# The last stage's sums of weight blocks, made once in memory by negating copies and adding DMA

## The chip, the cores and the metric

The kernel runs on one core of a Trainium2 chip. The time is the device time of one execution in microseconds; the times before are 738.42, 739.38 and 739.89 us, with a median of 739.38. The profile comes from one further execution, which took 738.09 us.

## The reference

The output is a gated mix of two branches over the same input `x` (1 x 2048 x 1024, bf16). Branch a is attention over eight earlier positions, two apart, with 32 heads of 32; branch b is a GELU-gated two-matrix layer with 3584 hidden columns.

```
def _A_ref(x, wqkv, wo):                 # H = 32; Dh = D // H; W, dil = 8, 2
    qkv = (x @ wqkv).reshape(B, S, 3, H, Dh)
    ...
    logits = jnp.einsum("bhsd,bhswd->bhsw", q, kg) * scale
    logits = jnp.where(mask[None, None, :, :], logits, -1e9)
    attn = _softmax(logits, axis=-1)
    o = jnp.einsum("bhsw,bhswd->bhsd", attn, vg)
    return (lambda x, *d: x.transpose(*d))(o, 0, 2, 1, 3).reshape(B, S, D) @ wo

def _B_ref(x, w_gate, w_up, w_down):
    g = jnp.einsum("bsd,df->bsf", x, w_gate)
    u = jnp.einsum("bsd,df->bsf", x, w_up)
    h = _gelu(g) * u
    return jnp.einsum("bsf,fd->bsd", h, w_down)

x = A_x
g = _sigmoid((x * gate_w).sum(-1, keepdims=True))
a = _A_ref(x, A_wqkv, A_wo)
b = _B_ref(x, B_w_gate, B_w_up, B_w_down)
return g * a + (1 - g) * b
```

The kernel puts `g` and `1 - g` into the attention weights and into `h`, so that both branches end in one matrix product: `[h, o]` (2048 x 4608) times `[w_down; wo]` (4608 x 1024). This product is the last stage, and the change is about its right-hand side.

## The kernel before

**Products with seven instead of eight block multiplications.** Every large product is cut into 2 x 2 blocks and made with seven block products and sums of blocks (the Strassen-Winograd scheme). The sums of right-hand blocks in the last stage are T1 = R12 - R11, T2 = R22 - T1, T3 = R22 - R12 and T4 = R21 - T2. A block R11, R12, R21 or R22 is a half of the 36 row blocks of `[w_down; wo]` (14 of `w_down`, 4 of `wo`) by 512 of the 1024 columns: 128 partitions x 18 x 512 in bf16, 2.36 MB. The first digit says which half of the rows, the second which half of the columns.

**Unit stage.** 78 units (class `Unit`, lines 354 to 407) make the gate and up products, q, k and v. A unit is 28 matmuls of 128x512 on TensorE. The loop at line 1005 goes through the units and writes each engine's order by hand: `p1` of the unit, `p73` of the one before, `p5`, `p26`, `p4` of the one before, then the callbacks of that iteration (`at`, before; `at_end`, after), and then `run_bg`, which gives VectorE and the DMA queues pieces of background work (attention, sums, stores). Within a unit ScalarE copies X to Y (L378), keeps V (L383), writes the first quarter to the unit's tile (L366 Gelu or L368 copy), copies Y to Z (L390) and writes another quarter; a gate unit ends with a Gelu of the second half (L405). TensorE adds onto Y and Z, so it waits for L378 and L390.

**Tiles of the units.** Gate and up units take their tiles from a ring of five (`st_tile`, lines 218 to 221). When a pair of a gate and an up unit is done, VectorE multiplies the two tiles (L250) and GpSimd stores the gate's tile to `h_d` in memory (L254). Gate units have even numbers from 28 on. The store of units n and n+1 is written in iteration n+3, and unit n+5 takes the same tile.

**Queues.** SP issues nearly all loads, in the order in which the program writes them. GpSimd issues the stores to `h_d`, `o_d`, `w_d` and others, likewise in order. A DMA that has to wait for data holds back what is behind it on its queue.

**Last stage.** `down(s)` runs twice, for 1024 rows of the output each time (s = 0, 1). A pass has seven block products of 72 matmuls each (L904) in this order: A11 x R11, A12 x R21, S x T1, S x T2, A12 x R22, A11 x T3, A22 x T4, where the left-hand blocks A and S are scaled and combined by VectorE (L831, L838, L950). The right-hand sums are made on VectorE by `comb_task` (L838): T1 over R11, T2 in a buffer of its own, T3 over R12, T4 (with a minus sign) over R21. `plan` says which of ten arena buffers of 18 KB each block lies in, for each pass. The four blocks R11, R21, R12 and R22 are loaded anew in the second pass (`loads_1` to `loads_6`). R11 is first loaded by a callback at unit 62 (`n - 16`), R21 while attention ends. The outputs of the first pass go out on GpSimd's queue, those of the second on SP's.

**The arena.** One tile holds everything in SBUF, by offsets in KB. 92 to 120 is used by the v projection's weights and sums until unit 25, and from unit 62 on by the last stage's buffers.

Of the kernel before, what the change touches and what calls it, by code (L numbers as in the profile page):

```python
# [46 lines left out]
R_ST = 178  # L47
R_P5B = 198.5
R_RAW = (0, 8)
R_S = (16, 24)  # L50
R_VB = 32
R_AB = 41
# [14 lines left out]
def kernel(  # L67
# [37 lines left out]
    def reg3(kb, a, b):  # L105
        return reg(kb, a * b).rearrange("p (a b) -> p a b", a=a)
# [14 lines left out]
    v_d = tc.dram_tile([P, NT, HALO + S], BF16, name="v_d")  # L121
    h_d = tc.dram_tile([P, 2 * NPAIR, S], BF16, name="h_d")
    o_d = tc.dram_tile([P, NT, S], BF16, name="o_d")
    z_d = tc.dram_tile([HK, S], F32, name="z_d")
    g_d = tc.dram_tile([2, S], BF16, name="g_d")
    w_d = tc.dram_tile([NBLK, 32, NJ, SC], BF16, name="w_d")
# [4 lines left out]
    with tc.manual_schedule(engines={mybir.EngineType.PE, mybir.EngineType.DVE, mybir.EngineType.Activation,  # L131
# [55 lines left out]
        def flat(a):  # L187
            return a.rearrange("p a b -> p (a b)")
# [605 lines left out]
        def load_A(b, s, half, c, i0, i1, with_o):  # L794
            t0 = s * SUP + c * SC
            nc.sync.dma_start(out=b[:, i0:i1, :], in_=h_src(half, t0, i0, i1))
            if with_o:
                nc.sync.dma_start(out=b[:, NH_:NK, :], in_=o_d[:, half * 4:half * 4 + 4, t0:t0 + SC])

        def h_src(half, t0, i0, i1):  # L800
            return h_d[:, :, t0:t0 + SC].rearrange("p (i two) s -> p i two s", two=2)[:, i0:i1, half, :]

        def load_R(b, half, nh):
            n0 = nh * SC
            nc.sync.dma_start(out=b[:, 0:NH_, :],
                              in_=B_w_down[:, n0:n0 + SC].rearrange("(i two p) n -> p i two n", two=2, p=P)[:, :, half, :])
            nc.sync.dma_start(out=b[:, NH_:NK, :],
                              in_=A_wo[:, n0:n0 + SC].rearrange("(p t) n -> p t n", t=NT)[:, 4 * half:4 * half + 4, :])

        plan = [dict(A11=4, R11=5, A12=2, R21=3, A21=6, A22=0, R12=1, R22=7, S=8, T2=9),  # L810
                dict(A11=6, R11=5, A12=8, R21=9, A21=2, A22=4, R12=7, R22=1, S=0, T2=3)]
        u2 = regf(R_U2, 4 * SC).rearrange("p (j n) -> p j n", j=4)
        qs = regf(R_QS, 4 * SC).rearrange("p (j n) -> p j n", j=4)
        on = [0]
# [8 lines left out]
        def Bs(s):  # L823
            return {k: bufs[v] for k, v in plan[s].items()}
# [9 lines left out]
        def comb_task(o_, a, b, op, step=4):  # L834
            for i0 in range(0, NK, step):
                i1 = min(NK, i0 + step)
                f = lambda t_: flat(t_[:, i0:i1, :])
                TT(out=f(o_), in0=f(a), in1=f(b), op=op)  # L838
                yield 0.05 + 0.273 * (i1 - i0)

        def run(*gens):
            for g in gens:
                for _ in g:
                    pass

        def pieces(*gens):
            for g in gens:
                yield from g

        def take(g, k):  # L850
            for _ in range(k):
                if next(g, None) is None:
                    break
# [19 lines left out]
        def loads_1(s):  # L873
            B = Bs(s)
            load_A(B["A11"], s, 0, 0, 0, NH_, True)
            load_R(B["R11"], 0, 0)

        def loads_2(s):
            B = Bs(s)
            load_A(B["A12"], s, 1, 0, 0, NH_, True)  # L880
            load_R(B["R21"], 1, 0)

        def loads_3(s):
            load_A(Bs(s)["A21"], s, 0, 1, 0, NH_, True)

        def loads_4(s):
            load_A(Bs(s)["A22"], s, 1, 1, 0, NH_, True)

        def loads_5(s):
            load_R(Bs(s)["R12"], 0, 1)  # L890

        def loads_6(s):
            load_R(Bs(s)["R22"], 1, 1)

        def down(s):
            B = Bs(s)
            last = s == 1
            eng = nc.sync if last else nc.gpsimd
            base = s * SUP
            XT, VT = (6, 7, 0, 1), (5, 2, 3, 4)  # L900

            def mm(ps, L, R, j, start, q0=0, q1=NK):
                for q, i in list(enumerate(KORD))[q0:q1]:
                    nc.tensor.matmul(ps, lhsT=L[:, i, j * P:(j + 1) * P], rhs=R[:, i, :], start=(start and q == 0),  # L904
                                     stop=(q == NK - 1), skip_group_check=not start)

            def emit(ot, c, nh, j):
                r0 = base + c * SC + j * P
                eng.dma_start(out=o2[r0:r0 + P, nh * SC:(nh + 1) * SC], in_=ot)

            def add_out(ps, t_, c, nh, j):
                ot = out_tile()
                TT(out=ot, in0=ps, in1=t_, op=ALU.add)  # L913
                emit(ot, c, nh, j)

            A11, A12, A21, A22 = B["A11"], B["A12"], B["A21"], B["A22"]
            R11, R12, R21, R22, S, T2 = B["R11"], B["R12"], B["R21"], B["R22"], B["S"], B["T2"]
            T1 = R11
            XP = [bank(XT[j]) for j in range(4)]
            VP = [bank(VT[j]) for j in range(4)]  # L920
            rest = pieces(scale_task(A21, s, 1, 0, NE_), scale_task(A22, s, 1, 0, NE_), comb_task(S, A21, A22, ALU.add))
            for j in range(4):
                if j > 1 or last:
                    mm(XP[j], A11, R11, j, True)
                else:
                    mm(XP[j], A11, R11, j, True, 0, NK - 2)
                    yield
                    if j == 1:
                        for jj in range(2):
                            mm(XP[jj], A11, R11, jj, True, NK - 2, NK)  # L930
                            nc.scalar.copy(out=u2[:, jj, :], in_=XP[jj])
                if j > 1 or last:
                    nc.scalar.copy(out=u2[:, j, :], in_=XP[j])  # L933
                take(rest, 3)
            run(rest)
            rest = comb_task(T1, R12, R11, ALU.subtract)
            for j in range(4):
                mm(XP[j], A12, R21, j, False)
                ot = out_tile()
                nc.scalar.copy(out=ot, in_=XP[j])  # L940
                emit(ot, 0, 0, j)
            run(rest)
            t2 = comb_task(T2, R22, T1, ALU.subtract)
            for j in range(4):
                mm(VP[j], S, T1, j, True)
                nc.scalar.copy(out=qs[:, j, :], in_=VP[j])
            run(t2)
            for j in range(4):
                js = slice(j * P, (j + 1) * P)
                TT(out=S[:, :, js], in0=S[:, :, js], in1=A11[:, :, js], op=ALU.subtract)  # L950
            run(comb_task(A12, A12, S, ALU.subtract), comb_task(A11, A11, A21, ALU.subtract))
            if not last:
                loads_1(1)
            rest = pieces(comb_task(R12, R22, R12, ALU.subtract), comb_task(R21, R21, T2, ALU.subtract))
            for j in range(4):
                mm(XP[j], S, T2, j, True)
                TT(out=u2[:, j, :], in0=XP[j], in1=u2[:, j, :], op=ALU.add)
                TT(out=qs[:, j, :], in0=qs[:, j, :], in1=u2[:, j, :], op=ALU.add)
                take(rest, 2)
            for j in range(4):  # L960
                mm(VP[j], A12, R22, j, False)
                add_out(VP[j], u2[:, j, :], 0, 1, j)
                take(rest, 1)
            run(rest)
# [12 lines left out]
            for j in range(4):  # L977
                mm(XP[j], A22, R21, j, False)
                add_out(XP[j], u2[:, j, :], 1, 0, j)
                take(rest, 1)  # L980
            run(rest)

        n = len(units)
# [2 lines left out]
        def run_last(b):  # L986
            now[0] = b
            prv = units[b - 1]
            for t_ in [t_ for t_ in tasks if t_.wake < b]:
                t_.finish()  # L990
            prv.p73()
            pre_down_3(0)
            loads_3(0)
# [66 lines left out]
```

## Time and profile before

| | |
|---|---|
| median of three runs | 739.38 us |
| profiled execution | 738.09 us |
| its span, first to last instruction | 736.3 us |
| TensorE busy | 724.4 us (98%) |
| VectorE busy | 589.6 us (80%) |
| ScalarE busy | 290.8 us (39%) |
| GpSimd busy | 91.3 us (12%) |
| DMA queue of SP (q1) | 77.41 MB, 34.4% of 16 engines' span |
| software DMA queue of GpSimd (q0) | 29.15 MB, 11.9% |
| granted TensorE clock | 1.000 |

The profile names engines PE (TensorE), DVE (VectorE), ACT (ScalarE), POOL (GpSimd) and SP. L904 means line 904 of the kernel before. Matmuls are pipelined and their ends are modelled, so the mean of one in a group (379 ns) is longer than the distance between two of them. The chain of waits is followed back from the last instruction: each step goes to what released it or to the instruction before it on its engine. The unit stage ends and the last stage begins around 517 us.

### The profile page before, as it was taken

The page shows a single profiled execution, that of the slowest core. Times are in us where ns is not written, and L with a number is a line of the kernel's source. Part 1 is how long each engine was busy: PE and PEld are TensorE (multiplying, and loading weights), DVE is VectorE, ACT ScalarE, POOL GpSimd, SP SyncE. Part 2 cuts the span into 40 slices and gives each one's busy share as a digit, 9 for nine tenths or more (in the row PEclk, how much of TensorE's full clock was granted, in tenths as well). Part 3 has the DMA queues.
Part 4 walks back from the last instruction along what each step waited for, and adds up shares of the span by engine and source line. Part 5 has one row for each costly group of instructions (what it writes and reads, how often), then busy time and mean ns, then how long its engine had stood idle before and what let it go on. Part 6 is the DMA issues. An engine that isn't in the chain of part 4 may idle for free.

```text
span 736.3 us, 9168 instructions
## 1 busy us (share of the span) xinstructions
PE 724.4 (98%) x3498; PEld 355.9 (48%) x3567; DVE 589.6 (80%) x626; ACT 290.8 (39%) x500; POOL 91.3 (12%) x160
## 2 busy tenths in 40 slices
PE   8999999999999999999999999999999999999998
PEld 4466665656544444444444444444444444444443
DVE  2697879878998899999999999986488944927921
ACT  4554445445566655555555555555110000110000
POOL 1222233411201100101001010000010011000000
PEclk9999999999999999999999999999999999999999
DMA  9972001362328334634346553637990899300011
GB/s 278 274 185 66 16 25 33 104 224 83 110 72 238 96 103 128 202 109 150 117 143 218 175 158 97 215 116 277 305 300 1 276 364 361 113 28 1 8 43 37
DMA packets 108333, 107.68 MB, mean 146 GB/s; under 512 B 17488, under 2 KB 95472, under 8 KB 108288
## 3 DMA queue, kind: packets, MB, share of 16 engines
q1 hardware_dynamic: 97856, 77.41, 34.4%
q0 software_dynamic: 10144, 29.15, 11.9%
q8 instruction: 28, 0.46, 0.3%
q10 hardware_dynamic: 288, 0.52, 0.3%
q14 instruction: 17, 0.14, 0.1%
HBM read 74.42 MB, written 30.55 MB: 143 GB/s over the span
## 4 chain that ended last, share of the span: by engine, by line
PE 81%; issue 1%; ACT 0%; DVE 0%
PE banks L360 51%; PE banks L904 29%; PE banks L596 1%; ACT L686 0%; DVE arena L913 0%; ACT arena L686 0%; ACT arena L366 0%; ACT banks L378 0%; ACT arena L405 0%
## 5 line engine op out<-in xcount | busy, mean ns | idle before, releaser
L360 PE MATMUL banks<-arena 128*128 128x512 bf16 x2137 | 472.2, 379 | 4.9 <-DVE arena L397 1.1
L360 PEld LDWEIGHTS <-arena 128*128 128x128 bf16 x2184 | 240.5, 111 | 236.1 <-issue 7.8
L904 PE MATMUL banks<-arena 128*128 128x512 bf16 x988 | 217.2, 379 | 1.1
L904 PEld LDWEIGHTS <-arena 128*128 128x128 bf16 x1008 | 98.6, 98 | 119.3 <-issue 0.6
L397 DVE TENSOR_TENSOR arena<-banks,arena 128x1024 bf16<-128x1024 f32 x78 | 95.2, 1221 | 39.3 <-PE banks L360 21.7
L383 ACT COPY arena<-banks 128x512 f32<-128x512 f32 x78 | 45.7, 586 | 130.9 <-PE banks L360 130.9
L730 DVE TENSOR_TENSOR arena<-arena 128x2048 bf16<-128x2048 bf16 x64 | 76.9, 1218 | 0.4
L368 ACT CAST arena<-banks 128x512 bf16<-128x512 f32 x102 | 59.7, 586 | 42.8 <-PE banks L360 42.8
L591 DVE TENSOR_TENSOR arena<-arena 128x2048 bf16<-128x2048 bf16 x64 | 74.7, 1218 | 0.1
L737 DVE TENSOR_TENSOR arena<-arena 128x2048 bf16<-128x2048 bf16 (+2 forms) x96 | 73.8, 775 | 1.1
L838 DVE TENSOR_TENSOR arena<-arena 128x2048 bf16<-128x2048 bf16 (+1 forms) x70 | 73.4, 1112 | 0.5 <-DMA arena<-in_B_w_down_dram 0.4
L913 DVE TENSOR_TENSOR arena<-banks,arena 128x512 bf16<-128x512 f32 x24 | 16.5, 690 | 47.6 <-PE banks L904 47.6
L390 ACT COPY banks<-banks 128x512 f32<-128x512 f32 x78 | 44.5, 571 | 22.1 <-PE banks L360 19.8
L254 POOL DMA_DIRECT2D h_d<-arena x28 | 20.1, 716 | 252.0 <-DVE arena L250 195.1
L378 ACT COPY banks<-banks 128x512 f32<-128x512 f32 x78 | 45.0, 577 | 13.8 <-PE banks L360 12.4
L317 DVE TENSOR_TENSOR arena<-arena 128x1024 bf16<-128x1024 bf16 x60 | 38.6, 685 | 0.5
L366 ACT ACTIVATE arena<-banks 128x512 bf16<-128x512 f32 x54 | 32.2, 597 | 15.2 <-PE banks L360 14.3
L250 DVE TENSOR_TENSOR arena<-arena 128x2048 bf16<-128x2048 bf16 x28 | 34.0, 1215 | 3.3 <-ACT arena L368 1.9
L831 DVE TENSOR_TENSOR arena<-arena,omgrep 128x2048 bf16<-128x2048 bf16 x24 | 28.1, 1217 | 10.4 <-DMA arena<-h_d 10.4
L933 ACT COPY arena<-banks 128x512 f32<-128x512 f32 x6 | 3.5, 586 | 81.8 <-PE banks L904 81.8
L950 DVE TENSOR_TENSOR arena<-arena 128x2304 bf16<-128x2304 bf16 x8 | 10.8, 1356 | 22.9 <-PE banks L904 20.3
L405 ACT ACTIVATE arena<-arena 128x1024 bf16<-128x1024 bf16 x27 | 28.3, 1049 | 0.0
(74 smaller groups left out, 256.8 us busy)
## 6 DMA issues: line engine op xcount, KB each, us to landing
h_d<-arena POOLq DMA_DIRECT2D x28, 512.0 KB, 4.0
arena<-in_B_w_down_dram SPq DMA_DIRECT2D x8, 1792.0 KB, 13.4
arena<-h_d SPq DMA_DIRECT2D x6, 1792.0 KB, 13.4
arena<-in_B_w_gate_dram SPq DMA_DIRECT2D x15, 512.0 KB, 5.2
arena<-in_B_w_up_dram SPq DMA_DIRECT2D x15, 512.0 KB, 4.3
arena<-in_A_wqkv_dram SPq DMA_DIRECT2D x6, 1024.0 KB, 10.8
arena<-v_d SPq DMA_DIRECT2D x8, 544.0 KB, 6.1
v_d<-arena POOLq DMA_DIRECT2D x16, 256.0 KB, 2.3
```

Of the source, the lines that this page charges most:

```text
L317: TT(out=o_, in0=a, in1=b_, op=op)
L360: self.pe = nc.tensor.matmul(ps, lhsT=self.L[form](kt), rhs=rhs[:, kt, :], start=(start and kt == 0), stop=(kt == HK - 1), skip_group_chec ...
L368: nc.scalar.copy(out=o_, in_=i_)
L378: nc.scalar.copy(out=self.Y, in_=self.X)
L383: nc.scalar.copy(out=self.p5s, in_=self.V)
L390: nc.scalar.copy(out=self.Z, in_=self.Y)
L397: TT(out=self.T[:, :, c2s], in0=pair, in1=self.p5s.rearrange("p (o n) -> p o n", o=1).to_broadcast([P, 2, SC]), op=ALU.add)
L591: TT(out=dst, in0=q.rearrange("p (o s) -> p o s", o=1).to_broadcast([P, NWIN, AC]), in1=_win_ap(k, [[-DIL, NWIN], [1, AC]]), op=ALU.mult)
L730: TT(out=prod2[(t // 2) % 2][:, t % 2], in0=ab, in1=_win_ap(v[:, t, HALO:HALO + AC], [[SJ, NJ], [-DIL, NWIN], [1, SJ]]), op=ALU.mult)
L737: TT(out=out_, in0=h(0), in1=h(1), op=ALU.add)
L838: TT(out=f(o_), in0=f(a), in1=f(b), op=op)
L904: nc.tensor.matmul(ps, lhsT=L[:, i, j * P:(j + 1) * P], rhs=R[:, i, :], start=(start and q == 0), stop=(q == NK - 1), skip_group_check=not ...
```

## The change

The four sums T1 to T4 are made once, in memory (`t_d`, four tensors of one block), during units 28 to 66, and both passes load them as blocks of their own.

- In units 28 to 54 SP loads the blocks R11, R12 and R22 in thirds (six row blocks, 0.786 MB) into four buffers at 92 to 116 KB of the arena. ScalarE negates them in place, 128x1024 at a time, one piece at the end of each of iterations 30 to 56. GpSimd stores the result: -R11 as the start of T1, -R12 as the start of both T2 and T3, -R22 as the start of T4.
- GpSimd then issues DMAs that add in memory: R12 to T1 (unit 41), R11 to T2 (50), R22 to T3 (52), R22 to T2 (56), R21 to T4 (60), each in two parts (`w_down` and `wo`), and at unit 66 T1 to T4.
- In the last stage the VectorE sums T1 to T4 and the load of R12 go away; T1 to T4 are loaded by SP. `plan` gives them buffers, and the loads of both passes are put at other places between the products.

```diff
+R_NEG = 92
+    t_d = [tc.dram_tile([P, NK, SC], BF16, name=f"t_d{k}") for k in range(4)]
...
+        def r_parts(half, nh, i0=0, i1=NK):
...
+        def load_T(b, k):
+            nc.sync.dma_start(out=b, in_=t_d[k - 1][:])
+
+        NP = 6
+        NQ = NK // NP
+        neg = [reg3(R_NEG + NP * q, NP, SC) for q in range(4)]
+
+        def neg_load(q, half, nh):
+            i0 = NP * (q % NQ)
+            for sl, src in r_parts(half, nh, i0, i0 + NP):
+                nc.sync.dma_start(out=neg[q % 4][:, sl.start - i0:sl.stop - i0, :], in_=src)
+
+        def neg_scale(q, r):
+            g = flat(neg[q % 4][:, 2 * r:2 * r + 2, :])
+            nc.scalar.activation(out=g, in_=g, func=ACT.Copy, scale=-1.0)
+
+        def neg_store(q, ks):
+            i0 = NP * (q % NQ)
+            for k in ks:
+                nc.gpsimd.dma_start(out=t_d[k - 1][:, i0:i0 + NP, :], in_=neg[q % 4])
+
+        def t_add(k, half, nh):
+            for sl, src in r_parts(half, nh):
+                nc.gpsimd.dma_start(out=t_d[k - 1][:, sl, :], in_=src, accum_op=ALU.add)
+
+        def t_add_t(k, k2):
+            nc.gpsimd.dma_start(out=t_d[k - 1][:], in_=t_d[k2 - 1][:], accum_op=ALU.add, max_dma_last_dim=2 * SC)
+
+        for q in range(3 * NQ):
+            half, nh, ks = ((0, 0, (1,)), (0, 1, (2, 3)), (1, 1, (4,)))[q // NQ]
+            at(28 + 3 * q, lambda q=q, half=half, nh=nh: neg_load(q, half, nh))
+            for r in range(3):
+                at_end(30 + 3 * q + r, lambda q=q, r=r: neg_scale(q, r))
+            at(33 + 3 * q, lambda q=q, ks=ks: neg_store(q, ks))
+        for n_, k, a in ((41, 1, (0, 1)), (50, 2, (0, 0)), (52, 3, (1, 1)), (56, 2, (1, 1)), (60, 4, (1, 0))):
+            at(n_, lambda k=k, a=a: t_add(k, *a))
+        at(66, lambda: t_add_t(4, 1))
...
-        plan = [dict(A11=4, R11=5, A12=2, R21=3, A21=6, A22=0, R12=1, R22=7, S=8, T2=9),
-                dict(A11=6, R11=5, A12=8, R21=9, A21=2, A22=4, R12=7, R22=1, S=0, T2=3)]
+        plan = [dict(A11=4, R11=5, A12=2, R21=3, A21=6, A22=0, S=8, T1=1, T2=9, R22=7, T3=5, T4=3),
+                dict(A11=6, R11=1, A12=8, R21=9, A21=2, A22=4, S=0, T1=7, T2=5, R22=3, T3=1, T4=9)]
...
-            rest = comb_task(T1, R12, R11, ALU.subtract)
+            loads(s, "T3")
             for j in range(4):
-                mm(XP[j], A12, R21, j, False)
+                mm(XP[j], A12, B["R21"], j, False)
...
-            run(rest)
-            t2 = comb_task(T2, R22, T1, ALU.subtract)
+            loads(s, "T4")
             for j in range(4):
-                mm(VP[j], S, T1, j, True)
+                mm(VP[j], S, B["T1"], j, True)
                 nc.scalar.copy(out=qs[:, j, :], in_=VP[j])
-            run(t2)
...
-                loads_1(1)
-            rest = pieces(comb_task(R12, R22, R12, ALU.subtract), comb_task(R21, R21, T2, ALU.subtract))
+                loads(1, "A11", "R11")
...
+                loads(1, "A12", "R21")
...
-                loads_2(1)
-                loads_3(1)
-                loads_5(1)
+                loads(1, "A21", "T1")
...
-                mm(XP[j], A11, R12, j, True)
+                mm(XP[j], A11, B["T3"], j, True)
...
-                loads_4(1)
-                loads_6(1)
+                loads(1, "A22", "T2")
...
+            if not last:
+                loads(1, "R22")
...
-            loads_4(0)
-            loads_5(0)
-            loads_6(0)
+            loads(0, "A22", "T1", "T2", "R22")
```

More of the change, by code (lines that the diff above doesn't have):

```diff
@@ L801, in h_src @@
             return h_d[:, :, t0:t0 + SC].rearrange("p (i two) s -> p i two s", two=2)[:, i0:i1, half, :]
-        def load_R(b, half, nh):
[L804 to L808, printed above, removed]
@@ L810 @@
-        plan = [dict(A11=4, R11=5, A12=2, R21=3, A21=6, A22=0, R12=1, R22=7, S=8, T2=9),
-                dict(A11=6, R11=5, A12=8, R21=9, A21=2, A22=4, R12=7, R22=1, S=0, T2=3)]
+        def r_parts(half, nh, i0=0, i1=NK):
+            ns = slice(nh * SC, (nh + 1) * SC)
+            if i0 < NH_:
+                e = min(i1, NH_)
+                yield slice(i0, e), B_w_down[:, ns].rearrange("(i two p) n -> p i two n", two=2, p=P)[:, i0:e, half, :]
+            if i1 > NH_:
+                a = max(i0, NH_)
+                yield slice(a, i1), A_wo[:, ns].rearrange("(p t) n -> p t n", t=NT)[:, 4 * half + a - NH_:4 * half + i1 - NH_, :]
@@ new lines, in load_R @@
+        def load_R(b, half, nh):
+            for sl, src in r_parts(half, nh):
+                nc.sync.dma_start(out=b[:, sl, :], in_=src)
+        def load_T(b, k):
[7 more added lines that the diff above has]
+                nc.sync.dma_start(out=neg[q % 4][:, sl.start - i0:sl.stop - i0, :], in_=src)
@@ new lines, in neg_scale @@
+        def neg_scale(q, r):
[6 more added lines that the diff above has]
+        def t_add(k, half, nh):
+            for sl, src in r_parts(half, nh):
+                nc.gpsimd.dma_start(out=t_d[k - 1][:, sl, :], in_=src, accum_op=ALU.add)
@@ L871, in pre_down_3, with loads @@
                 load_A(B[k], s, half, 0, NE_, NH_, False)
-        def loads_1(s):
+        def loads(s, *names):
             B = Bs(s)
[L875 to L893, printed above, removed]
+            for k in names:
+                if k[0] == "A":
+                    load_A(B[k], s, int(k[2]) - 1, int(k[1]) - 1, 0, NH_, True)
+                elif k[0] == "R":
+                    load_R(B[k], int(k[1]) - 1, int(k[2]) - 1)
+                else:
+                    load_T(B[k], int(k[1]))
         def down(s):
@@ L914, in add_out @@
                 emit(ot, c, nh, j)
-            A11, A12, A21, A22 = B["A11"], B["A12"], B["A21"], B["A22"]
-            R11, R12, R21, R22, S, T2 = B["R11"], B["R12"], B["R21"], B["R22"], B["S"], B["T2"]
-            T1 = R11
+            A11, A12, A21, A22, S = B["A11"], B["A12"], B["A21"], B["A22"], B["S"]
             XP = [bank(XT[j]) for j in range(4)]
@@ L923, in down @@
                 if j > 1 or last:
-                    mm(XP[j], A11, R11, j, True)
+                    mm(XP[j], A11, B["R11"], j, True)
                 else:
-                    mm(XP[j], A11, R11, j, True, 0, NK - 2)
+                    mm(XP[j], A11, B["R11"], j, True, 0, NK - 2)
                     yield
@@ L929, in down @@
                         for jj in range(2):
-                            mm(XP[jj], A11, R11, jj, True, NK - 2, NK)
+                            mm(XP[jj], A11, B["R11"], jj, True, NK - 2, NK)
                             nc.scalar.copy(out=u2[:, jj, :], in_=XP[jj])
@@ L952, in down @@
             if not last:
-                loads_1(1)
-            rest = pieces(comb_task(R12, R22, R12, ALU.subtract), comb_task(R21, R21, T2, ALU.subtract))
+                loads(1, "A11", "R11")
             for j in range(4):
-                mm(XP[j], S, T2, j, True)
+                mm(XP[j], S, B["T2"], j, True)
                 TT(out=u2[:, j, :], in0=XP[j], in1=u2[:, j, :], op=ALU.add)
                 TT(out=qs[:, j, :], in0=qs[:, j, :], in1=u2[:, j, :], op=ALU.add)
-                take(rest, 2)
+            if not last:
+                loads(1, "A12", "R21")
             for j in range(4):
-                mm(VP[j], A12, R22, j, False)
+                mm(VP[j], A12, B["R22"], j, False)
                 add_out(VP[j], u2[:, j, :], 0, 1, j)
-                take(rest, 1)
-            run(rest)
+            rest = pieces()
             if not last:
-                loads_2(1)
-                loads_3(1)
-                loads_5(1)
+                loads(1, "A21", "T1")
                 rest = pieces(scale_task(Bs(1)["A11"], 1, 0, 0, NE_), scale_task(Bs(1)["A12"], 1, 0, 0, NE_))
             for j in range(4):
-                mm(XP[j], A11, R12, j, True)
+                mm(XP[j], A11, B["T3"], j, True)
                 add_out(XP[j], qs[:, j, :], 1, 1, j)
@@ L974, in down @@
             if not last:
-                loads_4(1)
-                loads_6(1)
+                loads(1, "A22", "T2")
             for j in range(4):
-                mm(XP[j], A22, R21, j, False)
+                mm(XP[j], A22, B["T4"], j, False)
                 add_out(XP[j], u2[:, j, :], 1, 0, j)
                 take(rest, 1)
+            if not last:
+                loads(1, "R22")
             run(rest)
@@ L992, in run_last @@
             pre_down_3(0)
-            loads_3(0)
+            loads(0, "A21")
             first = down(0)
```

## The prediction

> **What bounds the kernel now.** I read the chain of waits first, then the groups for the last stage's lines, then the pieces of the chain where anything but TensorE stands in it, then the DMA busy share by stretch, then ScalarE and GpSimd in order of time.
>
> The page's chain and groups (group columns: busy us, mean ns of one, then idle us just before the group and who ended it):
>
> ```profile
> PE banks L360 51%; PE banks L904 29%; PE banks L596 1%; ACT L686 0%; DVE arena L913 0%; ACT arena L686 0%; ACT arena L366 0%; ACT banks L378 0%; ACT arena L405 0%
> ...
> L904 PE MATMUL banks<-arena 128*128 128x512 bf16 x988 | 217.2, 379 | 1.1
> ...
> L838 DVE TENSOR_TENSOR arena<-arena 128x2048 bf16<-128x2048 bf16 (+1 forms) x70 | 73.4, 1112 | 0.5 <-DMA arena<-in_B_w_down_dram 0.4
> ```
>
> TensorE is the bound, in the unit stage (L360) and in the last stage (L904) alike. Over the last stage's 217.2 us of matmuls TensorE stood idle 1.1 us. The VectorE sums of weight blocks are inside the 70 rows of L838; no matmul of L904 waits for them. The one place where ScalarE is on the chain after 129 us is this (start, length, what):
>
> ```profile
> 245.70 0.60 ACT arena L366
> 246.29 0.28 ACT arena L405
> 246.57 0.67 issue
> 247.24 1.28 ACT L686
> 248.53 0.01 issue
> 248.54 0.63 ACT arena L686
> 249.17 0.49 ACT banks L378
> ```
>
> There an Exp needs a table load (L686, 1.28 us), L378's copy comes late and TensorE waits 0.59 us.
>
> Busy time by stretch (the last two columns are the DMA share and GB/s):
>
> ```profile
> 343.00:368.00 25.00, 24.84 (x115) 11.33 (x117) 24.45 (x29) 14.05 (x24) 1.75 (x3) 1.00 0.43 128
> 368.00:380.00 12.00, 11.95 (x55) 5.45 (x56) 11.33 (x12) 6.59 (x12) 1.56 (x2) 1.00 0.54 178
> ...
> 600.00:620.00 20.00, 19.89 (x92) 9.01 (x93) 9.11 (x10) 0.00 (x0) 2.71 (x5) 1.00 1.09 361
> ```
>
> The last line is a full DMA system: 361 GB/s at a share of 1.09. So 1 MB costs 2.77 us of it, and a share of 0.43 is 0.39 of what there is. GpSimd in order of time, and one ScalarE row:
>
> ```profile
> 342.62 0.72 POOL L254 DMA_DIRECT2D h_d<-arena  x1 [3.67 <-DVE arena L250]
> 354.50 0.71 POOL L254 DMA_DIRECT2D h_d<-arena  x1 [11.16 <-DVE arena L250]
> 367.21 0.71 POOL L254 DMA_DIRECT2D h_d<-arena  x1 [12.01 <-DVE arena L250]
> ```
>
> ```profile
> 365.59 0.58 ACT L368 CAST arena<-banks 128x512 bf16<-128x512 f32 x1 [0.28 <-PE banks L360]
> ```
>
> GpSimd stores a gate tile about every 12 us. Five tiles rotate, so the tile of unit 48, stored at 354.50, is written again by unit 53, whose first evacuation is the row at 365.59. That is 11.1 us after the issue; the store lands in 4.0 us in the median. In before nobody waits there.
>
> **The change part by part.**
>
> *Sums taken off VectorE.* Eight of them (four in each pass), each four pieces of 1.218 us and one of 0.681: 5.55 us, 44.4 us in all. TensorE waits for none, so the gain is between 0 and the 1.1 us of idle before L904; I take 0.
>
> *Loads of the last stage.* Each pass loads seven weight blocks where it loaded four, six more in all, 2.36 MB each (2.25 x 1.049), 6.5 us of full DMA. In the first pass T1 takes R12's place in SP's queue, which before was issued at 529.5 and landed some 13.4 us later, at 543; T1 is wanted by the third product, at 548.6, and now needs no VectorE sum behind it. T2 and R22 follow at 6.5 us each (550 and 556; wanted at 564 and 580, a product being 72 matmuls of 0.219 us = 15.8), then T3 and T4 (about 563 and 570; wanted at 596 and 611). In the second pass the last load, R22, waits for the first pass's end (627) and is wanted at 689. SP's queue holds only loads there until the outputs of the second pass. The margin is 7 us or more everywhere but at T1 (5.6), and before's R12 was later in effect. Taken: 0. If a load were one 6.5 us block late, T1 would cost about 1 us.
>
> *Negating copies on ScalarE.* 27 of 128x1024 bf16. The row of that size is L405's Gelu, 1.049 us: 28.3 us, one in each of iterations 30 to 56. L515, a scaled copy before, ran in 0.21 us with no table load beside it, so none is added. Behind each stands the next unit's L378, whose result the unit's S2 matmuls want. After a gate unit L378 ran at 259.97 to 260.56 and is wanted at 262.8; 1.05 later is 261.6. After an up unit there is 2.1 us left by the same reckoning. Hidden, except in iteration 33, which is the stretch at 245.7 shown above: there the copy lies on the chain, **+1.0 us** (0 to 1.05). Without the cover it would be 28.
>
> *Negated loads and stores.* Nine loads and twelve stores of 0.786 MB, 2.2 us of full DMA each, one unit apart or more, issued two units or more before the work that uses them. GpSimd issues 12 stores and 11 adding DMAs; its rows cost 0.5 to 0.9 us each, so 12 to 20 us on an engine that is 12% busy. Taken: 0 by themselves, but they count in the budgets below.
>
> *Adding DMAs.* Five read 2.36 MB of weights and one a sum; each adds into a sum in memory. No row of before shows an adding DMA. From below: only what is written counts, 2.36 MB at 361 GB/s, 6.5 us. From above: a slower row, a 512 KB load from w_d in 4.6 us (114 GB/s), for the source and for the old destination: 41 us. I take **13.1 us**: source and old sum are both read, 4.72 MB at 361 GB/s. It is nearest to the rows of the big loads, whose runs of 1 KB are the same.
> The Trainium skill (Collectives: The Full Stack, "The bandwidth ceiling: the fold count and why AG ≠ RS ≠ AR") says that a reducing transfer is half as fast as a copy, since it has two sources to read, and not for the add itself. By that rule an add is 13.1 us and the sum is the one below; by the single pass it would be +1. No trace here shows it.
>
> What they cost hangs on the queue they are in. The page has one software queue (q0) for all that GpSimd issues, and I assume that it is served in order. A gate-tile store behind an add lands only when the add is through. If it lands after the next evacuation wants the tile, ScalarE stands, and with it L390's copy, for which TensorE has about 2.3 us (L390 starts at 366.45, TensorE wants it at 369.05 after twelve matmuls, the copy takes 0.57). So each add has a budget from the store before it to 2.3 us behind the evacuation that wants the store after it. Existing DMA work is the stretch's share over 1.09 times its length.
> - Add at unit 41: 282.7 to 307.4, 24.7 us. Existing share 0.42: 9.5; the add 13.1; a negated load 2.2. 24.8: nothing over.
> - Unit 50: 343.4 to 367.9, 24.5. Share 0.43: 9.7; 13.1; a negated store and a load 4.4. 27.2: 2.7 over.
> - Unit 52: 12.1 more, to 380.0. Share 0.54: 6.0; 13.1. 19.1: 7.0 over.
> - Unit 56: 379.4 to 404.1, 24.7. Share 0.51: 11.6; 13.1; one store 2.2. 26.9: 2.2 over.
> - Unit 60: 403.8 to 428.3, 24.5. Share 0.67 (the block R11 is loaded here): 15.1; 13.1. 28.2: 3.7 over.
> - Unit 66: 440 to 464.6. Share 0.36: 8.1; 13.1. 21.2 of 24.6: nothing.
> Together 15.6 us. A stall moves all that follows, so the overruns add up.
>
> **Sum:** 15.6 + 1.0 = +16.6 on the profiled execution's 738.09 (span 736.3 and 1.8 around it), 754.7. The median of the runs is 739.38, 1.3 above it; on the median it is **756**. An add of 6.5 us leaves only the unit-52 place with 0.4 over: 740 to 741. One of 21 us is 7.9 more in each of the six: 8.0, 10.6, 14.9, 10.1, 11.6 and 4.5, together 59.7, so 800 on the median. At 41 us it would be some 180 us.
>
> **Rivals.**
> 1. *All of it is hidden; not slower.* The adds run at one pass, or the stores don't queue behind them. For it: half of the DMA is free from 280 to 440, and chained adds are 4 to 10 units apart. Against: two adds 12 us apart beside a share of 0.43 to 0.54. Time: 739.4 + 1.0, so 739.4 to 740.9 with the 0.4 above.
> 2. *The adds are far slower than two passes*, the read of the old sum and its write standing one behind the other. Every gate store behind an add is then late, VectorE's weight sums and the SP loads too; from about 21 us each it is 800 and more. Against: the sums in a memory as wide as this should stream as loads do.
> 3. *Faster.* The idle before L904 goes with VectorE's sums, and ScalarE's copy at 245.7 finds cover: 739.4 - 1.1 = 738.3, with luck 737.5. Against: the chain has no VectorE sum in it.
>
> **How the numbers follow.** Forecast 0.50 (742 to 785 by itself), rival 1 0.24, rival 2 0.20, rival 3 0.06. What can be told from no change is 0.2%, 1.5 us. Faster by more 0.06, within it 0.24, slower 0.70. The range, 738.5 to 800, holds the forecast, rival 1 and the near end of rival 2.
>
> **What would show it.** ScalarE's evacuations (L366, L368) waiting for a DMA h_d<-arena, near units 43, 53, 55, 59 and 63; landing times of the h_d stores well over 4 us behind the adds; adds landing in 13 to 25 us from issue; no wait of L904 for a load; 1 us more at 245.7. Wrong if the adds land in under 10 us (rival 1) or over 30 (rival 2), if the store behind an add lands ahead of it, or if TensorE waits for a T block in the last stage.

## The result and the profile after

The changed kernel takes 761.95 us in the median (759.48 to 764.02), against 739.36 before: a ratio of 1.031, with a 95% interval of 1.027 to 1.034. The profiled execution has a span of 759.6 us, 23.3 more than before's 736.3. The change makes the kernel about 3% slower. One of the four executions of experiment 9 below took 1994.5 us and is left out of its figures.

The page of the changed kernel, with its chain and its groups (columns as in the prediction; L362 is now the units' matmul, L938 the last stage's, L319 the sums of gate and up weights):

```profile
q0 software_dynamic: 25872, 52.75, 25.7%
...
PE 70%; DMA 6%; DVE 5%; ACT 1%; issue 1%; DVEq 0%; ACTq 0%
PE banks L362 40%; PE banks L938 29%; DMA arena<-in_B_w_up_dram 6%; DVE arena L739 1%; DVE arena L399 1%; DVE arena L319 1%; DVE arena L732 1%; PE banks L598 1%; ACT arena L832 0%; ACT L688 0%; ACT arena L407 0%; ACT banks L392 0%; DVE arena L252 0%; ACT arena L368 0%; ACT banks L380 0%
...
L362 PE MATMUL banks<-arena 128*128 128x512 bf16 x2184 | 479.3, 381 | 21.3 <-ACT banks L392 10.0
...
L938 PE MATMUL banks<-arena 128*128 128x512 bf16 x1008 | 217.9, 379 | 0.0
```

The loss is in the unit stage. TensorE waits for nothing in the last stage: 0.0 us idle before L938. The 1.1 us that before's page shows there were probably no wait either: that trace holds only 988 of the stage's 1008 matmuls and names no wait for them. Nine of the experiments' traces hold 988 too and show 1.0 to 1.4 us more idle than the waits they name; the three with 1008 (the changed kernel, 11 and 12) show none. The chain, which was TensorE nearly from end to end, now holds DMA at 6%: loads of the up weights. The DMA engines are near their limit for long: from 285 to 480 us their share is 1.02, and from 345 to 420 it is 1.01 to 1.17, where the same stretch of before has 0.19 to 0.83. The waits (us in total, times, longest) name two kinds:

```profile
ACT arena L370 <- DMA h_d<-arena: 15.3, 3, 8.8
DVE arena L319 <- DMA arena<-in_B_w_up_dram: 11.5, 4, 3.9
PE banks L362 <- ACT banks L392: 10.0, 4, 7.1
PE banks L362 <- DVE arena L399: 9.0, 9, 2.4
```

ScalarE's evacuation L370 waits until a gate tile is stored, and with it L392, for which TensorE waits. VectorE's L319 waits for a load of up weights, and behind it stands L399, for which TensorE waits too. Here the load issued at 302.02 took 14.9 us, and the sums started when it had landed:

```profile
317.06 2.62 DVE L319 TENSOR_TENSOR arena<-arena 128x1024 bf16<-128x1024 bf16 x4 [3.89 <-DMA arena<-in_B_w_up_dram]
```

TensorE in order of time shows where (start, length, ..., in brackets the idle time before):

```profile
250.89 58.00 PE L362 MATMUL banks<-arena 128*128 128x512 bf16 x268 [1.55 <-ACT banks L380]
309.96 10.83 PE L362 MATMUL banks<-arena 128*128 128x512 bf16 x48 [1.07 <-ACT banks L392]
323.14 12.25 PE L362 MATMUL banks<-arena 128*128 128x512 bf16 x56 [2.35 <-DVE arena L399]
...
395.50 13.04 PE L362 MATMUL banks<-arena 128*128 128x512 bf16 x48 [7.10 <-ACT banks L392]
...
449.65 34.69 PE L362 MATMUL banks<-arena 128*128 128x512 bf16 x160 [1.17 <-ACT banks L392]
486.63 51.10 PE L362 MATMUL banks<-arena 128*128 128x512 bf16 x236 [2.29 <-DVE arena L399]
```

The longest, 7.10 us, can be followed through GpSimd's queue and ScalarE:

```profile
360.96 2.03 POOL L841 DMA_DIRECT2D t_d<-in_B_w_down_dram  x1
362.10 2.19 POOL L841 DMA_DIRECT2D t_d<-in_A_wo_dram  x1
374.63 0.75 POOL L256 DMA_DIRECT2D h_d<-arena  x1 [10.35 <-DVE arena L252]
```

```profile
394.37 0.59 ACT L370 CAST arena<-banks 128x512 bf16<-128x512 f32 x1 [8.80 <-DMA h_d<-arena]
```

The add's two parts, issued at 361 and 362, take 28.1 and 30.7 us to land, because the add of unit 50 is still ahead of them. The gate store issued at 374.63 takes 19.7 us, to 394.3, and L370 starts at 394.37. Of TensorE's four waits for L392 the last, 1.17 us at 449.65, has the same cause, though the profile puts this evacuation's wait down to TensorE:

```profile
448.53 0.59 ACT L370 CAST arena<-banks 128x512 bf16<-128x512 f32 x1 [2.87 <-PE banks L362]
```

The store of that tile, issued at 434.89 behind the add of unit 60, took 13.6 us, to 448.49. The DMA issues by line (KB each, median us to landing), first in before, then in the changed kernel:

```profile
h_d<-arena POOLq DMA_DIRECT2D x28, 512.0 KB, 4.0
arena<-in_B_w_up_dram SPq DMA_DIRECT2D x15, 512.0 KB, 4.3
```

```profile
h_d<-arena POOLq DMA_DIRECT2D x28, 512.0 KB, 6.7
...
t_d<-in_B_w_down_dram POOLq DMA_DIRECT2D x5, 1792.0 KB, 19.1
...
arena<-in_B_w_up_dram SPq DMA_DIRECT2D x15, 512.0 KB, 7.3
```

The idle pieces of TensorE from 240 to 540 us add up so: behind gate stores 1.07 + 0.70 + 7.10 + 1.17 = 10.0; behind L399, which I put down to the up weights, 2.35 + 0.33 + 1.12 + 1.12 + 0.53 + 2.29 = 7.7; at the Exp at 246 us 1.55 where it was 0.59, 1.0. Behind the 7.10 us TensorE also ran at a lower granted clock (the column after PEld's, here 0.89 and 0.53; then DMA share and GB/s):

```profile
388.00:395.50 7.50, 0.40 (x3) 0.10 (x1) 2.41 (x3) 1.13 (x3) 3.05 (x2) 0.89 1.12 317
395.50:401.00 5.50, 5.50 (x14) 2.00 (x14) 1.22 (x1) 3.04 (x5) 0.00 (x0) 0.53 1.11 295
```

14 matmuls in 5.5 us where 25 fit: 5.5 x 0.47 = 2.6 us. Together 21.3 of the 23.3 us; the rest I did not place.

### The profile page after: what moved, and what is told of

The parts are those of the page before. It is cut to its first block, busy times and chain, and to the rows that moved or that the text cites. A ratio compares the mean times of both kernels' runs of the same rounds, so it can differ in the third digit from the quotient of the medians.

```text
span 759.6 us, 9297 instructions
## 1 busy us (share of the span) xinstructions
PE 731.7 (96%) x3567; PEld 355.9 (47%) x3567; DVE 549.4 (72%) x586; ACT 314.5 (41%) x527; POOL 117.4 (15%) x183
## 3 DMA queue, kind: packets, MB, share of 16 engines
q0 software_dynamic: 25872, 52.75, 25.7%
## 4 chain that ended last, share of the span: by engine, by line
PE 70%; DMA 6%; DVE 5%; ACT 1%; issue 1%; DVEq 0%; ACTq 0%
PE banks L362 40%; PE banks L938 29%; DMA arena<-in_B_w_up_dram 6%; DVE arena L739 1%; DVE arena L399 1%; DVE arena L319 1%; DVE arena L732 1%; PE banks L598 1%; ACT arena L832 0%; ACT L688 0%; ACT arena L407 0%; ACT banks L392 0%; DVE arena L252 0%; ACT arena L368 0%; ACT banks L380 0%
## 5 line engine op out<-in xcount | busy, mean ns | idle before, releaser
L362 PE MATMUL banks<-arena 128*128 128x512 bf16 x2184 | 479.3, 381 | 21.3 <-ACT banks L392 10.0
L362 PEld LDWEIGHTS <-arena 128*128 128x128 bf16 x2184 | 241.1, 111 | 259.0 <-issue 33.5
L938 PE MATMUL banks<-arena 128*128 128x512 bf16 x1008 | 217.9, 379 | 0.0
L938 PEld LDWEIGHTS <-arena 128*128 128x128 bf16 x1008 | 98.6, 98 | 118.9
L399 DVE TENSOR_TENSOR arena<-banks,arena 128x1024 bf16<-128x1024 f32 x78 | 95.2, 1221 | 51.0 <-PE banks L362 31.9
L370 ACT CAST arena<-banks 128x512 bf16<-128x512 f32 x102 | 59.8, 586 | 60.0 <-PE banks L362 44.7
L392 ACT COPY banks<-banks 128x512 f32<-128x512 f32 x78 | 44.6, 572 | 27.6 <-PE banks L362 17.3
L319 DVE TENSOR_TENSOR arena<-arena 128x1024 bf16<-128x1024 bf16 x60 | 38.7, 686 | 12.0 <-DMA arena<-in_B_w_up_dram 11.5
L884 DVE TENSOR_TENSOR arena<-arena 128x2048 bf16<-128x2048 bf16 (+1 forms) x30 | 31.2, 1111 | 0.1
## 6 DMA issues: line engine op xcount, KB each, us to landing
arena<-h_d SPq DMA_DIRECT2D x6, 1792.0 KB, 13.9
```

Source lines behind the costliest of these rows:

```text
L319: TT(out=o_, in0=a, in1=b_, op=op)
L362: self.pe = nc.tensor.matmul(ps, lhsT=self.L[form](kt), rhs=rhs[:, kt, :], start=(start and kt == 0), stop=(kt == HK - 1), skip_group_chec ...
L370: nc.scalar.copy(out=o_, in_=i_)
L392: nc.scalar.copy(out=self.Z, in_=self.Y)
L399: TT(out=self.T[:, :, c2s], in0=pair, in1=self.p5s.rearrange("p (o n) -> p o n", o=1).to_broadcast([P, 2, SC]), op=ALU.add)
```

## The experiments

All are timed against the kernel before on the same chip (738.7 to 739.7 us) and numbered in the order in which they ran; 4 and 11 were executed once, for their traces.

**1. No adds.** The six adding DMAs left out.

```diff
-        for n_, k, a in ((41, 1, (0, 1)), (50, 2, (0, 0)), (52, 3, (1, 1)), (56, 2, (1, 1)), (60, 4, (1, 0))):
-            at(n_, lambda k=k, a=a: t_add(k, *a))
-        at(66, lambda: t_add_t(4, 1))
```

> Leaves out the six adding transfers (so T1 to T4 are only their negated parts); all else as in the changed kernel. If the adds make the loss, by holding up the gate-tile stores (about 12.6 us with the clock that is lost behind a stall) and the w_up loads (about 7.7 us): 740.4 us, that is before + 1.0, with the 1.0 at the Exp near 246 us and no evacuation waiting for h_d. If the negated loads, copies and stores make it: 755 us or more. If the last stage's six further loads make it: 760 us.

Measured: 738.3 us, ratio 0.9994 (0.998 to 1.000). Negated loads, ScalarE's copies, stores and the last stage's six further loads cost nothing together that shows, and VectorE without its 44 us of sums gains nothing that shows: within a few tenths of a per cent the adds are the whole loss. The 1.0 us at the Exp is in the trace; in the time it can't be told, since before's executions beside this run spread from 737.6 to 740.7. Its page:

```profile
q0 software_dynamic: 11872, 38.59, 15.1%
...
PE 81%; ACT 1%; issue 0%; DVE 0%
```

**2. Plain copies for the adds.** The same bytes on the same queue, without the addition.

```diff
-                nc.gpsimd.dma_start(out=t_d[k - 1][:, sl, :], in_=src, accum_op=ALU.add)
+                nc.gpsimd.dma_start(out=t_d[k - 1][:, sl, :], in_=src)
...
-            nc.gpsimd.dma_start(out=t_d[k - 1][:], in_=t_d[k2 - 1][:], accum_op=ALU.add, max_dma_last_dim=2 * SC)
+            nc.gpsimd.dma_start(out=t_d[k - 1][:], in_=t_d[k2 - 1][:], max_dma_last_dim=2 * SC)
```

> The six adding transfers become plain copies of the same blocks on the same queue at the same places (T1 to T4 are then the last block copied). If the price of an add is that source and old sum are both read, a copy is half of it, lands in 8 to 12 us in place of 19 to 22, and the time is 741 to 747 us. If a transfer of that size in GpSimd's queue costs the same whatever it does: 758 us or more. If the addition itself is slow: 740 to 741 us with copies landing in under 8 us.

Measured: 738.45 us, ratio 0.9994 (0.998 to 1.001). The copies landed in 8.9 to 13.9 us, near the 8 to 12 expected of half the price, but the time fell all the way, below the expected 741. The share of the DMA engines from 285 to 480 us is 0.83, where the adds made it 1.02. No evacuation waited for a store. The page's software queue and the row of the copies:

```profile
q0 software_dynamic: 15504, 52.75, 20.2%
...
t_d<-in_B_w_down_dram POOLq DMA_DIRECT2D x5, 1792.0 KB, 10.9
```

From the three pages' q0 rows the price follows: 15.1% of 736.6 is 111.2 us of the 16 engines without adds, 20.2% of 736.5 is 148.8 with copies, 25.7% of 759.6 is 195.2 with adds. A copy of 2.36 MB is 6.3 us, an add 14.0, or 2.2 copies. The Trainium skill's rule (Collectives: The Full Stack, "The bandwidth ceiling: the fold count and why AG ≠ RS ≠ AR"), that a reduction between cores has two sources to read and is half as fast as a copy, comes near it.

**3. Seven tiles in the ring.** A gate store may be two units later before an evacuation wants its tile.

```diff
         def st_tile():
-            k = st_n[0] % 5
+            if st_n[0] == 22:
+                st_ring[0:0] = [R_PROD, R_PROD + 4]
+            if st_n[0] == 48:
+                st_ring[:] = [r for r in st_ring if r >= R_ST]
...
+            st_ring.append(st_ring.pop(0))
+            return reg3(st_ring[-1], 2, SUP)
```

> The ring of gate and up tiles has seven places in place of five in units 40 to 65 (8 KB at 84 KB of the arena, free there); all else as in the changed kernel, adds too. If evacuations that wait for a late gate store cost about 12.6 us of the 22.6: 748 to 751 us, no evacuation waits for h_d, and the waits of VectorE's weight sums for w_up stay. If the loss is the loads alone: 760 to 763 us. If both are one and the same delay, seen twice: 755 to 762 us, with the w_up waits growing.

Measured: 778.44 us, ratio 1.054 (1.049 to 1.058), slower than all that was expected. No evacuation waited for h_d. VectorE's weight sums waited 23.8 us for up weights, and the last stage's third product 11.1 us for VectorE. This second wait came from the tiles that the last units got: experiment 5 puts these back and it is gone. Why those places were late was not tried.

**4. The add by itself.** Two adds and a copy of 1.84 MB in a quiet stretch of the kernel before.

```diff
+            src = B_w_down[:, 0:SC].rearrange("(i two p) n -> p i two n", two=2, p=P)[:, :, 0, :]
+            nc.gpsimd.dma_start(out=c_d[:], in_=src, **(dict(accum_op=ALU.add) if add else {}))
```

> The kernel before, with one plain copy (unit 6) and two adds (units 10 and 14) of a w_down half block, 1.84 MB, from memory to memory on GpSimd's queue, where the DMA engines are nearly idle; the time itself says nothing. Two reads for each write: the copy lands in 5.1 us + 2, the adds in 10.2 us + 2. One pass: both the same. Read and write one behind the other: adds of 25 us or more.

Measured: 8.8 us from issue to landing for the copy, 15.5 and 14.3 for the adds. The copy is 1.7 us over what was expected, the adds are 3.3 and 2.1 over what was expected of two reads for each write, and far from one pass or from 25 us. By these times an add alone is 1.6 to 1.8 copies; the 2.2 above is time of packets beside other traffic.

**5. Seven tiles, with the last units' places as in the changed kernel.** The edit against experiment 3:

```diff
-                st_ring[:] = [r for r in st_ring if r >= R_ST]
+                st_ring[:] = [R_ST + 4 * (k % 5) for k in range(48, 53)]
```

> The ring of seven tiles again, but from unit 66 on in the same order of places as in the changed kernel, so that the 11.1 us wait in the last stage of the first such run falls away. If late gate stores and late w_up loads are two covers over one delay of the DMA engines: 760 to 768 us, no evacuation waits for h_d, and VectorE's weight sums wait about 24 us for w_up. If the gate stores cost by themselves: 748 to 751.

Measured: 764.61 us, ratio 1.034 (1.031 to 1.037), as the changed kernel. Its waits:

```profile
PE banks L371 <- DVE arena L408: 21.3, 8, 12.2
DVE arena L328 <- DMA arena<-in_B_w_up_dram: 19.6, 3, 13.3
```

Of the gate stores none is left; the whole loss has gone over to the up weights (L328 is the weight sum here). Taking away the waits for gate stores alone gives nothing back.

**6. Weight sums one unit later, ring of five.** The opposite cover.

```diff
-            t_ = bg(sums_pair(w, sm), 1, max(n0 - 2, lo))
+            t_ = bg(sums_pair(w, sm), 1, max(n0 - 1, lo))
```

> As the changed kernel, but a pair's weight sums may start on VectorE one unit (6 us) later, so a late w_up load holds VectorE up to 6 us less; ring of five. If each w_up wait costs by itself: 762 - 7.7 = 754 us. If the two covers lie over one delay, what is gained here is lost again at the gate stores: 757 to 762. If the later sums are late for TensorE: above 762.

Measured: 766.47 us, ratio 1.037 (1.034 to 1.040). That is above 762, which was given for sums that come late for TensorE. The trace has no such wait in the unit stage: no weight sum waits for its load, TensorE waits for none of them, and the loss has gone over to the gate stores; 2.7 us more is a wait of the last stage for rows of h_d (see 10). The waits for the gate stores:

```profile
ACT arena L370 <- DMA h_d<-arena: 22.7, 4, 6.9
PE banks L362 <- ACT banks L392: 16.1, 4, 5.5
```

**7. Adds in pieces.** The same six adds in pieces of three of the 18 row blocks, one piece in each of units 36 to 74 (`t_add` takes a range of row blocks; pieces of one sum's rows at least four units apart).

```diff
-        def t_add(k, half, nh):
-            for sl, src in r_parts(half, nh):
+        def t_add(k, half, nh, i0, i1):
+            for sl, src in r_parts(half, nh, i0, i1):
```

> The same six adds with the same sums and the same bytes, each in six pieces of 0.39 MB, one piece in each of units 36 to 74. If the loss is the length of one add (14 us of the DMA engines) in front of gate stores and beside w_up loads: 739 to 743 us, h_d stores landing in at most 9 us and w_up loads in at most 9. If it is the total work of the DMA (adds 84 us on a system that is half busy): 750 to 762.

Measured: 751.2 us, ratio 1.018 (1.012 to 1.025). The four executions spread from 749.0 to 759.5. About half the loss is gone, and the gate stores' waits with it; stores and up weights still land in up to 14.5 and 14.9 us, not the expected 9, and VectorE waits 11.2 us for the up weights. The time lies in the span given for total work, but the same work in short pieces spread over more units costs less than in six long ones, so length, or the spread, counts too.

**8. Shorter runs.** Each add of weights in two DMAs of half the columns, 512-byte runs.

```diff
+                for c in range(0, SC, SC // 2):
+                    nc.gpsimd.dma_start(out=t_d[k - 1][:, sl, c:c + SC // 2], in_=src[:, :, c:c + SC // 2], accum_op=ALU.add)
```

> Each adding DMA of weights is issued as two, one for each half of the 512 columns, so that its runs are 512 bytes in place of 1 KB; same bytes and places. If a w_up load is slow beside an add because each run of the add holds an engine for long and the two queues take turns run by run: w_up lands in 7 to 12 us where it took 12.3 to 21.9, and the time is 748 to 758 us. If what counts is the engines' total work, which shorter runs make longer: 765 to 785 us, w_up as late or later.

Measured: 780.08 us, ratio 1.055 (1.051 to 1.059). Each side of the expectation is half right. The longest load of up weights came down from 21.9 to 13.4 us; at 301 us, where the two kernels still run alike, the load beside the first add took 10.3 us in place of 14.9. So SP's queue seems to come in oftener when the adds' runs are short; how, the trace does not show. But the adds grew to (28.0% of 778.9 - 111.2) / 6 = 17.8 us each on average, and the gate stores behind them waited:

```profile
ACT arena L370 <- DMA h_d<-arena: 38.6, 4, 11.6
```

**9 and 11. Both covers at once.** Seven tiles as in 5 and weight sums as in 6.

```diff
-            t_ = bg(sums_pair(w, sm), 1, max(n0 - 2, lo))
+            t_ = bg(sums_pair(w, sm), 1, max(n0 - 1, lo))
...
+            if st_n[0] == 22:
+                st_ring[0:0] = [R_PROD, R_PROD + 4]
```

> Both covers widened at once: seven tile places (in the order of the fifth experiment) and weight sums that may start one unit later; the six adds whole and where the change has them. If late gate stores and late w_up loads are two thresholds over one delay, each enough to stop TensorE, only both together give the time back: 740 to 748 us, with at most one wait for h_d or w_up left. If the engines' total work is the bound, or a third wait stands behind: 755 or more.

Measured: 753.5 to 756.1 us in three executions, the middle one 755.72, ratio 1.022 (1.019 to 1.024): 9 to 11 us less than with either cover alone, but 8 above the span expected of both, and in the span given for the engines' total work or a third wait. The same kernel once more, for its trace:

> The ninth experiment again for its trace, since its profiled execution was a disturbed one; its timed runs were 753.5 to 756.1 us, 9 to 11 below either cover alone. If what is left is w_up loads over 18 us late, one or two waits of VectorE's weight sums beside adds at units 52 to 56, together 8 to 12 us. If a third cover gives way: waits of another kind (attention's loads, the last stage's first loads of h_d) of that size.

It took 757.3 us. There is no third wait of that size: VectorE's waits for up weights, 13.1 us, are a little over the 8 to 12 expected, and the last stage's wait for h_d is 2.7. What is left, as expected, is two loads of up weights, too long for the wider cover too; the longest took 24.3 us. That leaves the engines' work of the two explanations, and shows it no further. The wait, and the first of the loads in the chain:

```profile
DVE arena L328 <- DMA arena<-in_B_w_up_dram: 13.1, 2, 7.2
```

```profile
374.44 24.26 DMA arena<-in_B_w_up_dram
```

**10. Pieces, and weight sums one unit later.**

```diff
-            t_ = bg(sums_pair(w, sm), 1, max(n0 - 2, lo))
+            t_ = bg(sums_pair(w, sm), 1, max(n0 - 1, lo))
...
+        def t_add(k, half, nh, i0, i1):
+            for sl, src in r_parts(half, nh, i0, i1):
```

> The adds in 36 pieces (as in the seventh experiment, where evacuations no longer waited for h_d and only the w_up waits, 11.2 us, were left) and the weight sums one unit later. If those w_up waits are what is left of the loss: 739 to 743 us. If the pieces make gate stores late as soon as VectorE no longer waits, as whole adds did in the sixth: 748 to 755.

Measured: 744.0 us, ratio 1.006 (1.005 to 1.008), one above the expected span of 739 to 743. Whole adds with this later start took 766.5 (experiment 6), pieces without it 751.2 (experiment 7). Its waits:

```profile
DVE arena L319 <- DMA arena<-in_B_w_up_dram: 2.8, 2, 2.5
PE banks L953 <- DMA arena<-h_d: 2.7, 1, 2.7
PE banks L362 <- ACT banks L380: 1.6, 1, 1.6
```

The second of these, the last stage waiting for rows of h_d, is there in the traces of 6, 10, 11 and 12, the ones with later weight sums, and in no other with the places of the tiles as in the change; so it seems to belong to that edit and not to the adds; the edit without adds was not tried.

**12. Four adds.** T2 starts as a copy of R11 and takes T3; T4 is T2 - R21.

```diff
-            half, nh, ks = ((0, 0, (1,)), (0, 1, (2, 3)), (1, 1, (4,)))[q // NQ]
+            half, nh, ks = ((0, 1, (3,)), (0, 0, (1,)), (1, 0, (4,)))[q // NQ]
...
+            at(30 + m, lambda i0=i0: t_copy(2, 0, 0, i0, i0 + PC))
```

> The same four sums with four adds in place of six: T2 starts as a plain copy of R11 and takes T3, T4 is kept with the other sign (T2 - R21, starting as -R21) and taken off at the output; nine negated stores in place of twelve. Adds and the copy in pieces of 0.39 MB, one in a unit, and the weight sums one unit later, as in the tenth experiment. Adds cost the engines 4 x 14 = 56 us in place of 84. If their work beside the loads is the whole of the loss: 738 to 741 us, no wait for h_d or w_up over 1 us. If adds cost by their mere presence: 742 to 745, as with six.

As run, the product with T4 was subtracted together with the product with T3, which lies in the same bank, so one quarter of the output differs; the work is the same. Measured: 742.66 us, ratio 1.0045 (1.003 to 1.006), 1.7 above the span of 738 to 741 expected if the adds' work were all, and in the 742 to 745 given for a cost of their mere presence. The trace speaks against that second reading: no wait for a gate tile or an up weight is left in the unit stage. What remains is the Exp's 1.0 us and this, 3.3 of the 3.9 us above before's 738.78:

```profile
PE banks L960 <- DMA arena<-h_d: 2.3, 1, 2.3
```

No version beats the kernel before, and experiment 1 shows why: with the adds left out the time is the same. Adds in the quiet early stretch of experiment 4 were not tried as a version of the change.

## Why the prediction was right

It said 756 us in a range of 738.5 to 800; 761.95 was measured. It named the right cause, the adds, and one of the two ways in which they cost. That its number came within 6 us is in part luck: one term was too large and another was missing. By its own steps:

- *TensorE is the bound and VectorE's sums are worth nothing.* Right within the noise: experiment 1. The 1.1 us of idle that the third rival hoped to gain was probably records that the trace lacks.
- *The last stage's loads, 0.* Right: 0.0 us idle before L938.
- *ScalarE's copies, 1.0 at 246 us and else nothing.* Right in the trace (0.59 to 1.55).
- *An add is 13.1 us, between 6.5 and 41.* 14.0 on the engines. Two reads for each write was the right choice, and experiment 2 shows that the lower end would indeed have cost nothing. The 361 GB/s that it divides by is not a ceiling: experiment 2 moved 382 from 300 to 320 us. From issue to landing the parts took 14.6 to 30.7 us, where 13 to 25 was named; the 28.1 and 30.7 of unit 52 lie above that, the last one over the 30 set as the second rival's mark, because another add was ahead of them. By time on the engines that rival fails all the same.
- *GpSimd's queue is served in order, and a gate store behind an add lands late.* Right: four stores behind adds landed 1.4 to 3.8 us after the add's last part. Of the five places named, evacuations waited at four, near units 43, 53, 55 and 63, the last by the landing time shown above.
- *The budgets: 15.6 us over, at units 50, 52, 56 and 60.* 10.0 us of idle behind gate stores. Add by add (41, 50, 52, 56, 60): 1.07, 0.70, 7.10, 0 and 1.17, where 0, 2.7, 7.0, 2.2 and 3.7 were forecast. The pair 12 us apart is what costs, as forecast; of the others the first was sized too low, the rest too high. That 7.10 meets 7.0 proves little beside these. The 2.6 us of low clock behind the longest were not foreseen.
- *The term that was missing:* loads by SP were counted as work in the budgets and not as victims. VectorE's weight sums waited for the up weights, 7.7 us of idle. The prediction named that only under its second rival. Even its sixth add, at unit 66, for which it forecast nothing, has such a wait behind it, the 2.29 us at 486.63. Gate stores 5.6 under, clock 2.6 and these 7.7 over: 4.7 of the 6.0 us between forecast and result.
- *What the budgets did not say,* and experiments 5, 6 and 9 show: the two waits are not two prices that add up, so a budget for each add's gate stores is not a price by itself. Late stores and late loads are better read as two covers over one delay. While ScalarE stands, VectorE's loads catch up, and the other way round; this reading fits the three runs. Widening one cover moves the loss to the other (764.6 and 766.5 against 762), and only both together give some of it back (755.7).

The first rival fell to the price of an add; the second to the same number; the third to experiment 1.

## What to carry to other kernels

Before moving work off an engine, look whether the engine that bounds the kernel ever waits for it; here 44 us of VectorE's work were free. The 84 us of DMA work that took their place were not, in six big adds; in 36 pieces with one cover wider they cost 4.5 us. Price an adding DMA as two copies or a little more, and ask what is queued behind it and which prefetches run beside it, since a big one delays both. When two waits appear together, widen each cover alone and then both: if the loss only changes its name, look for a common cause under them.

## What the runs showed of the hardware

Beside adds four loads of 0.5 MB of up weights on SP's queue took 12.3, 13.0, 14.9 and 21.9 us, where the longest was 6.4 without adds (experiment 1, from 280 to 520 us) and 9.8 beside copies (experiment 2). While the slowest was open, from 381.5 to 403.4 us, SP's queue had only this load, a gate load and the rest of a v_d load under way, at most 1.6 MB or 75 GB/s, of the 266 GB/s that the engines moved. With the adds' runs halved a load took at most 13.4 (experiment 8). How the queues take turns was not measured further.

An adding DMA also cost GpSimd more to issue: 2.0 to 2.2 us for each part, where the same copy cost 0.8 to 1.1.

TensorE's granted clock was 0.50 from 395.4 to 400.4 us, after 7.1 us of idle, and 1.00 again from 401.4 on; after gaps of 1 to 2.4 us it stayed at 1.00. The Trainium skill (TensorE: Matmul & The Clock Gate, "Part 1: The HAM clock gate (the "warmup" mystery)") states half speed after an idle window of about 3.4 us, until the array has been busy for such a window again; the trace agrees in the depth, and its low stretch of busy matmuls, 5 us, is longer than one window.
